# Three batches of attention as one list of steps, and one quad's row sums moved from TensorE to VectorE

## The chip, the cores and the metric

The kernel runs on one core of a Trainium2 chip. The metric is device microseconds from launch to end; the profile gives the time from the first to the last instruction of one execution, called the span.

## The reference

Cosine attention over 8 batches, 12 heads, 448 positions and 64 features, and behind it a two-layer feed-forward block with an exact GELU on the 3584 x 768 result:

```python
q_n = q / (np.linalg.norm(q, axis=-1, keepdims=True) + 1e-06)
k_n = k / (np.linalg.norm(k, axis=-1, keepdims=True) + 1e-06)
scores = np.matmul(q_n, k_n.transpose(0, 1, 3, 2)) / tau
attn = np.exp(scores - scores.max(-1, keepdims=True))
attn = attn / (attn.sum(-1, keepdims=True) + 1e-09)
x = np.matmul(attn, v).transpose(0, 2, 1, 3).reshape(B * S, H * D)
h = x @ w_in                                  # 768 -> 2048
out = (0.5 * h * (1.0 + erf(h / sqrt(2)))) @ w_out    # 2048 -> 768
```

The kernel leaves the subtraction of the maximum out: scores of unit vectors divided by 0.1 stay small enough. Inputs and output are float32; the matrix products run in bfloat16 and add up in float32.

## The kernel before

Four heads are a *quad*: three quads a batch, 24 in all, numbered g. Heads lie in pairs on the 128 partitions, and the 448 positions are seven chunks c of 64. A *unit* is what is normalised at once: units 0 and 1 are the halves of quad 0, and unit u from 2 on is quad u - 1. `load_qk(g)` loads a quad's q and k, so unit 5 belongs to `load_qk(4)`.

For each unit: `square` (ScalarE or GpSimd), `reduce` to sums of squares (VectorE), `logs` and `roots` (ScalarE, a square root as exponential of half a logarithm), `inverses` (VectorE), `scale` (GpSimd, gives bfloat16), `transposes` (TensorE with `copies` by VectorE for units 0 to 4, a DMA transpose on SP's queue for the others). Units share their logs and roots in groups; from group 5 on a group is not a unit.

For each quad and chunk: `scores` (four 64x64 matmuls side by side in the array, tile `st`), `exps` (ScalarE, 896 columns, line 252), the sums over rows, and `values` (four matmuls a chunk, tile `o`). `visit(p)` is one chunk's scores and exponentials in bank pair p. The sums come in three ways: `sums`, matmuls against ones into tile `sm`, followed by `turned` and `inverted`; `folded`, additions by GpSimd into SBUF; and `gathered`, additions by VectorE into a bank pair; the last two are followed by `turned_all` and `inverted_all`. `spread` and `normalise` (VectorE) then give x, bfloat16.

For each batch: `first(b)` projects x with `w_in` (96 matmuls of 448 columns, tile `hp`) and applies `gelu` on ScalarE from each bank. The second product (tile `op`, 16 matmuls of 384 columns for each half row block) is cut into single matmuls, *pieces*, which the next batch's attention takes in between its own work; the 16th copies the bank out, and a finished block is stored from SP's queue.

A program order is written out by hand (`manual_schedule`): each engine and each queue runs its instructions in the order in which the code issues them. Buffers are reused in that order too: q and k have four, v two, PSUM two single banks (`mm`, taken in turn for `tp`, `sm`, `op` and some `hp`), two pairs `st0`, `st1`, and two more single banks that become a third pair after batch 0.

Batch 0's attention is a list (`attention_first`); those of batches 1 and 2 are branches in `attention(b, fill)`, with a list `parts` of how many pieces go into each place; the rest is one pattern. `late_copy`, before the change two plain lines, is a copy of one column of quad 0's last load by GpSimd, ahead of its first other work. `spin` matmuls are padding: TensorE computes something that nothing reads.

Of the kernel before, what the change touches and what calls it, by code (L numbers as in the profile page):

```python
# [9 lines left out]
F32 = mybir.dt.float32  # L10
# [6 lines left out]
def kernel(  # L17
# [108 lines left out]
    def load_qk(g):  # L126
        b, n = divmod(g, NQ)
        t = qkp.tile([128, 2, 2, C, D], F32, tag="qk", name=f"qk{g}")
        qk_t[g] = t
        for s0, s1 in ((0, 1), (1, 2)) if g == 0 else ((0, 2),):  # L130
            for i, src in enumerate((q, k)):
                eng = nc.scalar if g == 0 and s0 == 0 and i == 1 else nc.sync
                eng.dma_start(
                    out=t[:, i, s0:s1].rearrange("p s c d -> p s (c d)"),
                    in_=src[b, 4 * n + 2 * s0:4 * n + 2 * s1].rearrange(
                        "(s h) (p c) d -> (h p) s (c d)", h=2, c=C))
# [127 lines left out]

    def gathered(g, p):
# [58 lines left out]
    def values(g, chunks=range(C), p=None):  # L324
        for c in chunks:
            if c == 0 and g < NQ:
# [70 lines left out]
    def second_pieces(sb, t, ni):  # L397
        state = {}

        def mm(kf):  # L400
# [8 lines left out]
            if kf == KF - 1:  # L409
                nc.vector.tensor_copy(ot[:, ni * NH:(ni + 1) * NH], ps[:, :NH])  # L410
# [7 lines left out]
        return [lambda kf=kf: mm(kf) for kf in range(KF)]  # L418
# [46 lines left out]
    early = {}  # L465

# [5 lines left out]
    def attention_first():  # L472
        x_t[0] = xp.tile([128, KD, S], BF16, tag="x", name="x0")
        DV, AC, GP = nc.vector, nc.scalar, nc.gpsimd
        Q, K = 0, 1
        square(0, ((AC, Q),))
        square(0, ((AC, K),))
        reduce(0, Q)
        reduce(0, K)
        square(1, ((AC, Q),))  # L480
        upto(load_v, 1)
        logs(0)
        reduce(1, Q)
        roots(0)
        upto(load_wi, 1)
        square(1, ((AC, K),))
        inverses(0)
        square(2, ((AC, Q),))
        reduce(1, K)
        scale(0, ((GP, 1),))  # L490
        logs(1)
        reduce(2, Q)
        roots(1)
        scale(0, ((GP, 0),))
        spin(2)
        transposes(0, 1)
        square(2, ((AC, K),))
        inverses(1)
        spin(1)
        transposes(0, 0)  # L500
        square(3, ((AC, Q),))
        copies(0, 1)
        scale(1, ((GP, 0),))
        copies(0, 0)
        square(3, ((AC, K),))
        scale(1, ((GP, 1),))
        upto(load_qk, 5)
        spin(1)
        transposes(1, 0)
        reduce(2, K)  # L510
        scores(0, ((0, 0), (0, 1)))
        upto(load_v, 2)
        transposes(1, 1)
        copies(1, 0)
        logs(2)
        scores(0, ((0, 2), (0, 3)))
        roots(2)
        upto(load_wi, 2)
        exps(0, ((0, 0), (0, 1)))
        inverses(2)  # L520
        copies(1, 1)
        exps(0, ((0, 2), (0, 3)))
        spin(2)
        scores(0, ((0, 4), (0, 5)))
        scale(2, ((GP, 0),))
        reduce(3, Q)
        exps(0, ((0, 4), (0, 5)))
        spin(1)
        scores(0, ((1, 0), (1, 1)))
        reduce(3, K)  # L530
        exps(0, ((1, 0), (1, 1)))
        spin(1)
        scores(0, ((1, 2), (1, 3)))
        scale(2, ((GP, 1),))
        upto(load_qk, 6)
        transposes(2, 0)
        exps(0, ((1, 2), (1, 3)))
        sums(0, (0,))
        copies(2, 0)
        scores(0, ((1, 4), (1, 5)))  # L540
        logs(3)
        scores(0, ((0, 6), (1, 6)))
        roots(3)
        transposes(2, 1)
        exps(0, ((1, 4), (1, 5)))
        inverses(3)
        sums(0, (1,))
        scale(3, ((GP, 0),))
        copies(2, 1)
        sums(0, (2,))  # L550
        exps(0, ((0, 6), (1, 6)))
        sums(0, range(3, 5))
        scores(1, ((0, 0), (1, 0)))
        scores(1, ((0, 1), (1, 1)))
        sums(0, (5,))
        exps(1, ((0, 0), (1, 0)))
        sums(0, (6,))
        upto(load_wi, 3)
        transposes(3, 0)
        turned(0)  # L560
        exps(1, ((0, 1), (1, 1)))
        scores(1, ((0, 2), (1, 2)))
        values(0, (0,))
        scale(3, ((GP, 1),))
        upto(load_wi, 4)
        copies(3, 0)
        values(0, (1,))
        exps(1, ((0, 2), (1, 2)))
        values(0, (2,))
        scores(1, ((0, 3), (1, 3)))  # L570
        inverted(0)
        values(0, range(3, 5))
        spread(0, 1)
        values(0, (5,))
        exps(1, ((0, 3), (1, 3)))
        scores(1, ((0, 4), (1, 4)))
        values(0, (6,))
        spread(0, 0)
        sums(1, (0,))
        square(4, ((GP, K),))  # L580
        exps(1, ((0, 4), (1, 4)))
        sums(1, (1,))
        scores(1, ((0, 5), (1, 5)))
        normalise(0, 0)
        transposes(3, 1)
        exps(1, ((0, 5), (1, 5)))
        scores(1, ((0, 6), (1, 6)))
        copies(3, 1)
        sums(1, (2,))
        square(4, ((GP, Q),))  # L590
        square(5)
        upto(load_wo, 2)
        exps(1, ((0, 6), (1, 6)))
        sums(1, range(3, 5))
        normalise(0, 1)
        scores(2, ((0, 0), (1, 0)))
        sums(1, (5,))
        exps(2, ((0, 0), (1, 0)))
        sums(1, (6,))
        scores(2, ((0, 1), (1, 1)))  # L600
        turned(1)
        values(1, range(2))
        exps(2, ((0, 1), (1, 1)))
        values(1, (2,))
        scores(2, ((0, 2), (1, 2)))
        inverted(1)
        values(1, range(3, 5))
        spread(1, 0)
        values(1, (5,))
        exps(2, ((0, 2), (1, 2)))  # L610
        values(1, (6,))
        scores(2, ((0, 3), (1, 3)))
        sums(2, (0,))
        reduce(4, K)
        normalise(1, 0)
        exps(2, ((0, 3), (1, 3)))
        sums(2, (1,))
        scores(2, ((0, 4), (1, 4)))
        spread(1, 1)
        values(2, (0,))  # L620
        sums(2, (2,))
        exps(2, ((0, 4), (1, 4)))
        scores(2, ((0, 5), (1, 5)))
        normalise(1, 1)
        values(2, range(1, 3))
        exps(2, ((0, 5), (1, 5)))
        values(2, (3,))
        scores(2, ((0, 6), (1, 6)))
        exps(2, ((0, 6), (1, 6)))
        reduce(4, Q)  # L630
        spin(1)
        early[4] = mm_tile("hp0_4")[:, :S]
        w_in(0, early[4], 4, range(2))
        sums(2, range(3, 7))
        values(2, (4,))
        logs(4)
        turned(2)
        values(2, (5,))
        roots(4)
        values(2, (6,))  # L640
        inverted(2)
        inverses(4)
        scale(4)
        spread(2, 1)
        spread(2, 0)
        normalise(2, 1)
        normalise(2, 0)
        done.update({square: 6, reduce: 5, root: 5, scale: 5, transposes: 5})

# [49 lines left out]

    def attention(b, fill):
        fill = list(fill)
        if b == 1:
            parts = iter((20, 13, 14, 17, 16, 16))
        elif b == 2:
            parts = iter((22, 12, 12, 13, 11, 13, 11, 11, 11, 6, 6))
        elif len(fill) == 128:
            parts = iter((14, 22, 22, 26, 28, 16))
        else:  # L710
            parts = iter((14, 17, 13, 18, 18, 16))
# [28 lines left out]
        if b == 1:  # L740
            upto(scale, u + 3)
            upto(load_v, b + 2)
            upto(transposes, u + 3)
            upto(load_qk, g0 + NQ + 2)
            upto(square, u + 4)
            visit(0, 1, 2)
            run()
            visit(0, 1, 2)
            run()
            upto(load_qk, g0 + NQ + 3)  # L750
            visit(0, 1)
            upto(square, u + 5)
            run()
            visit(0, 1, 2)
            both(g0, 0)
            upto(load_v, b + 3)
            upto(load_qk, g0 + NQ + 4)
            visit(1, 2)
            upto(reduce, u + 4)
            run()  # L760
            visit(1, 2, 0)
            both(g0 + 1, 1)
            visit(2, 0)
            logs(6)
            roots(6)
            run()
            both(g0 + 2, 2)
            inverses(6)
            done[root] = 7
        elif b == 2:  # L770
            upto(scale, u + 3)
            upto(load_qk, g0 + 6)
            upto(transposes, u + 3)
            upto(scale, u + 4)
            upto(load_qk, g0 + 7)
            upto(transposes, u + 4)
            visit(0, 1, 2)
            run()
            visit(0, 1, 2)
            norms(9)  # L780
# [230 lines left out]
```

## Time and profile before

| | |
|---|---|
| times of three runs | 402.37, 400.3, 406.49 us (median 402.37) |
| span of the profiled execution | 398.6 us |
| its own time | not among the three; the lowest run is 1.7 us above its span |
| TensorE, VectorE, ScalarE, GpSimd busy | 98, 66, 67, 63% |
| granted TensorE clock | 0.999 |

A row of the costliest groups reads: line, engine, operation, written tile <- read tiles, shapes, count | busy us, mean ns of one | idle us of that engine just before them, and what ended most of that. Rows of the chain are start, length, what. In a timeline the bracket at a row's end says how long the engine was idle before it, and for what.

### The profile page before, as it was taken

What the parts mean: (1) busy time and instruction counts of PE and PEld (TensorE: products, weight loads), DVE (VectorE), ACT (ScalarE), POOL (GpSimd) and SP (SyncE); (2) the same over time, 40 slices, a digit from 0 to 9 for tenths busy, and PEclk for the clock granted to TensorE, in tenths of its full rate; (3) what the DMA queues carried; (4) which work ended last, traced back from release to release, by engine and by line L of the source; (5) the groups of instructions that cost most, each with busy time, mean ns of one, the idle gap of its engine ahead of it and who ended that gap; (6) DMA issues with size and microseconds to landing.
All of it is one profiled execution on the core that took longest, in us unless ns stands there. A gap on an engine that the chain in (4) does not pass through costs nothing.

```text
span 398.6 us, 8027 instructions
## 1 busy us (share of the span) xinstructions
PE 392.0 (98%) x3245; PEld 207.8 (52%) x3245; DVE 264.0 (66%) x530; ACT 267.8 (67%) x399; POOL 250.6 (63%) x162
## 2 busy tenths in 40 slices
PE   7999999999999999999999999999999999999996
PEld 3444555555545555555555555555555555555564
DVE  5787214955487999589963999769973797461021
ACT  6995787557988877888665977889656756504300
POOL 5898814269699694959587394969768391920000
PEclk9999999999999999999999999999999999999999
DMA  8999999747296890678145591566024720130033
GB/s 290 261 258 217 205 233 308 154 106 226 50 254 234 158 230 2 178 150 207 70 105 138 126 240 38 162 113 147 2 27 101 148 46 2 41 77 3 1 80 80
DMA packets 66485, 54.52 MB, mean 137 GB/s; under 512 B 38672, under 2 KB 62352, under 8 KB 66448
## 3 DMA queue, kind: packets, MB, share of 16 engines
q1 hardware_dynamic: 54464, 41.79, 39.0%
q0 software_dynamic: 11600, 11.80, 18.8%
q8 instruction: 25, 0.41, 0.4%
q10 hardware_dynamic: 384, 0.43, 0.3%
q14 instruction: 12, 0.10, 0.1%
HBM read 45.61 MB, written 11.01 MB: 142 GB/s over the span
## 4 chain that ended last, share of the span: by engine, by line
PE 95%; issue 1%; DVE 1%; POOL 1%; ACT 0%; POOLq 0%
PE hp L469 37%; PE op L406 36%; PE st L242 9%; PE o L320 4%; PE o L335 4%; PE op L425 1%; PE sm L305 1%; PE sh L667 1%; PE tp L221 1%; PE sm L314 1%; PE spin L463 0%; POOL wi L441 0%; DVE nq L168 0%; POOL qkb L204 0%; POOL v L145 0%
## 5 line engine op out<-in xcount | busy, mean ns | idle before, releaser
L252 ACT ACTIVATE pt<-st 128x896 bf16<-128x896 f32 x155 | 132.5, 916 | 29.0 <-PE st L242 28.4
L406 PE MATMUL op<-wo,g 128*128 128x384 bf16 x864 | 148.1, 326 | 0.0
L469 PE MATMUL hp<-x,wi 128*128 128x448 bf16 x768 | 147.0, 353 | 0.1
L204 POOL TENSOR_TENSOR qkb<-qk,rn 128x896 bf16<-128x896 f32 (+1 forms) x50 | 80.2, 1628 | 66.3 <-DVE rn L188 64.9
L406 PEld LDWEIGHTS <-g 128*128 128x128 bf16 x864 | 81.4, 98 | 62.6 <-issue 11.2
L469 PEld LDWEIGHTS <-wi 128*128 128x128 bf16 x768 | 74.4, 98 | 71.1 <-issue 2.8
L263 POOL TENSOR_TENSOR acc<-acc,pt 128x896 f32<-128x896 f32 x55 | 103.8, 1887 | 4.3
L929 ACT ACTIVATE g<-hp 128x448 bf16<-128x448 f32 x128 | 63.6, 552 | 63.6 <-PE hp L469 63.5
L410 DVE COPY ot<-op 128x384 f32<-128x384 f32 x54 | 29.9, 555 | 83.1 <-PE op L406 80.8
L168 DVE TENSOR_REDUCE nq<-sq 128x14 f32<-128x896 f32 (+1 forms) x50 | 50.6, 1038 | 10.2 <-POOL sq L160 6.7
L242 PE MATMUL st<-qkT 64*64 64x448 bf16 x620 | 46.0, 356 | 0.2 <-ACT pt L252 0.2
L160 POOL TENSOR_TENSOR sq<-qk 128x896 f32<-128x896 f32 x18 | 29.9, 1683 | 16.3 <-DMA qk<-in_q_dram 10.9
L369 DVE TENSOR_TENSOR x<-o,rs 128x448 bf16<-128x448 f32 x48 | 28.0, 609 | 9.9 <-PE sh L667 6.4
L270 DVE TENSOR_TENSOR acc<-acc,pt 128x896 f32<-128x896 f32 x30 | 33.0, 1099 | 1.0
L158 ACT ACTIVATE sq<-qk 128x896 f32<-128x896 f32 (+1 forms) x32 | 27.8, 902 | 2.2 <-DMA qk<-in_q_dram 1.8
L364 DVE STREAM_TRANSPOSE rs<-rc 128x448 f32<-128x448 f32 x48 | 28.7, 626 | 0.6
L242 PEld LDWEIGHTS <-qkT 64*64 64x64 bf16 x620 | 17.9, 105 | 20.5 <-issue 12.7
L263 POOL TENSOR_TENSOR acc<-pt 128x896 f32<-128x896 bf16 x11 | 20.7, 1879 | 8.9 <-DVE x L369 8.9
L320 PE MATMUL o<-pt,v 64*64 64x448 bf16 x364 | 24.2, 351 | 0.0
L673 ACT ACTIVATE pt<-sh 128x448 bf16<-128x448 f32 x26 | 14.1, 544 | 9.2 <-PE sh L667 8.5
L276 DVE STREAM_TRANSPOSE ta<-acc 128x448 f32<-128x448 f32 x32 | 18.5, 617 | 0.2
L335 PE MATMUL o<-pt,v 64*64 64x448 bf16 x308 | 17.5, 351 | 0.5 <-DVE x L369 0.5
(54 smaller groups left out, 212.4 us busy)
## 6 DMA issues: line engine op xcount, KB each, us to landing
qk<-in_q_dram SPq DMA_DIRECT2D x23, 448.0 KB, 4.6
qk<-in_k_dram SPq DMA_DIRECT2D x23, 448.0 KB, 5.4
out_dram<-ot SPq DMA_DIRECT2D x48, 192.0 KB, 3.2
v<-in_v_dram POOLq DMA_DIRECT2D x7, 672.0 KB, 7.7
wo<-in_moe_w_out_dram POOLq DMA_DIRECT2D x4, 768.0 KB, 11.6
wi<-in_moe_w_in_dram POOLq DMA_DIRECT2D x4, 512.0 KB, 14.4
out_dram<-ot SPq DMA_DIRECT2D x12, 96.0 KB, 2.1
wi<-in_moe_w_in_dram POOLq DMA_DIRECT2D x4, 256.0 KB, 14.6
```

The source lines that it names most:

```text
L160: eng.tensor_tensor(sq, t, t, ALU.mult)
L168: nc.vector.tensor_reduce(nq_t[n][:, j, i], sq_t[g, i][:, s0:s1], mybir.AxisListType.X, ALU.add)
L204: eng.tensor_tensor(qkb[:, i, :, s0:s1].rearrange("p c s d -> p s c d"), t[:, i, s0:s1], rn[:, i].to_broadcast([128, s1 - s0, C, D]), ALU. ...
L242: nc.tensor.matmul(st[cols, n, :S], lhsT=qkT[rows, 1, c, cols], rhs=qkT[rows, 0, :, cols], start=True, stop=True, tile_position=(64 * s, 6 ...
L252: nc.scalar.activation(pt, st[:, :, :S], AF.Exp, scale=inv_tau)
L263: nc.gpsimd.tensor_tensor(acc_t[g], all_t[g][:, 0] if c == 1 else acc_t[g], all_t[g][:, c], ALU.add)
L270: nc.vector.tensor_tensor(acc_t[g], acc_t[g], all_t[g][:, c], ALU.add)
L320: nc.tensor.matmul(bank_t[g, h][64 * s:64 * (s + 1), :S], lhsT=v_t[g][rows, s, c, :], rhs=pt_t[g, s, c][rows], start=(c == 0), stop=(c == ...
L335: nc.tensor.matmul(bank_t[g, h][cols, :S], lhsT=v_t[g][rows, s, c, :], rhs=pt_t[g, s, c][rows], start=(c == 0), stop=(c == C - 1), tile_po ...
L406: nc.tensor.matmul(ps[:, :NH], lhsT=g_t[sb][:, kf, t * 128:(t + 1) * 128], rhs=wo[:, kf, ni * NH:(ni + 1) * NH], start=(kf == 0), stop=(kf ...
L469: nc.tensor.matmul(t, lhsT=wi[:, kd, m * 128:(m + 1) * 128], rhs=x_t[b][:, kd, :], start=(kd == 0), stop=(kd == KD - 1))
L929: nc.scalar.activation(g_t[sb][:, m, hf * S:(hf + 1) * S], hps.pop(m), AF.Gelu)
```

## The change

Batches 0, 1 and 2 up to `first(2)` become one list, `opening()`; `first(0)`, `first(1)` and the branches for batches 1 and 2 go, and the remaining code loses what only they used. What the list changes for the engines:

- `sums(3)`, the row sums of quad 3 by TensorE, becomes `gather(3, c)`, six VectorE additions into an SBUF tile, with `turned_all` and `inverted_all`.
- 8 of 14 copies of `op` banks in batches 1 and 2 go from VectorE to ScalarE (`run(1, AC)`).
- Squares: unit 1 from ScalarE to GpSimd; unit 5, one half each of units 6, 7, 9 and 10 from GpSimd to ScalarE; one half of unit 13 the other way.
- GpSimd's queue: the parts of `w_in`, issued before the scaling of quads 0, 1 and 2, go behind it; `late_copy` goes from the front to behind `load_wi(2)`; `load_v(4)` comes ahead of `load_v(3)`.
- SP's queue: `load_qk(10)` before 9 and 8, and stores in other places.
- The chunks of quads 0 to 2 come in another order, single matmul groups of batches 1 and 2 in other places; the 29 `spin` matmuls are placed one by one but for one run of 20; the two matmuls `early` are no longer taken ahead.

```diff
+    def gather(g, c):
+        if c == 1:
+            acc_t[g] = sqp.tile([128, 2, S], F32, tag="sq", name=f"acd{g}")
+        nc.vector.tensor_tensor(acc_t[g], all_t[g][:, 0] if c == 1 else acc_t[g], all_t[g][:, c], ALU.add)
...
-        def mm(kf):
+        def mm(kf, eng):
...
-                nc.vector.tensor_copy(ot[:, ni * NH:(ni + 1) * NH], ps[:, :NH])
+                (nc.scalar.copy if eng is nc.scalar else nc.vector.tensor_copy)(ot[:, ni * NH:(ni + 1) * NH], ps[:, :NH])
...
+    def run(n, eng=nc.vector):
+        for _ in range(n):
+            todo_t.pop(0)(eng)
...
+        square(1, ((GP, Q),))
...
+        scale(3, ((GP, Q),))
+        turned(0)
...
+        load_wi(2)
+        load_qk(4)
+        sums(1, (1,))
+        late_copy()
...
+        values(2, (3,))
+        values(2, (4,))
+        exps(2, ((0, 5), (1, 5)))
+        sums(2, (2,))
+        sums(2, (3,))
+        sums(2, (4,))
+        sums(2, (5,))
+        sums(2, (6,))
+        load_wi(3)
+        values(2, (5,))
+        values(2, (6,))
...
+        mm(0, 3, 0, 4)
...
+        table(GELU_SET)
+        bank(0, 5)
+        square(5, ((AC, K),))
+        mm(0, 4, 4, 6)
+        gelu(0, 4)
...
+        gather(3, 2)
+        run(1)
+        gather(3, 3)
+        gather(3, 4)
+        reduce(7, K)
+        gather(3, 5)
+        run(2)
+        gather(3, 6)
+        run(1)
+        run(1, AC)
...
+        sums(4)
+        turned(4)
...
+        load_v(4)
+        run(2)
+        table(GELU_SET)
+        inverted(5)
+        spread(5, 0)
+        load_v(3)
...
+        gelu(1, 13)
+        inverses(7)
+        bank(1, 11)
+        square(9, ((AC, Q),))
+        gelu(1, 12)
...
+    opening()
+    assert not todo_t, len(todo_t)
+    first(2)
+    for b in range(3, B):
+        attention(b, output_pieces(b - 1))
+        first(b)
```

## The prediction

> **What bounds the kernel now.** I read the page first: span, busy shares, the chain that ended last, the costliest groups.
>
> ```profile
> span 398.6 us, 8027 instructions
> PE 392.0 (98%) x3245; PEld 207.8 (52%) x3245; DVE 264.0 (66%) x530; ACT 267.8 (67%) x399; POOL 250.6 (63%) x162
> ...
> PE 95%; issue 1%; DVE 1%; POOL 1%; ACT 0%; POOLq 0%
> ...
> L252 ACT ACTIVATE pt<-st 128x896 bf16<-128x896 f32 x155 | 132.5, 916 | 29.0 <-PE st L242 28.4
> ...
> L929 ACT ACTIVATE g<-hp 128x448 bf16<-128x448 f32 x128 | 63.6, 552 | 63.6 <-PE hp L469 63.5
> L410 DVE COPY ot<-op 128x384 f32<-128x384 f32 x54 | 29.9, 555 | 83.1 <-PE op L406 80.8
> ```
>
> TensorE is 95% of the chain, and the other engines wait for it, not it for them. A busy TensorE need not be a fast one, so next the chain in order of time (start, length, what).
>
> ```profile
> 31.09 0.88 PE sm L305 x8
> 31.96 0.69 PE o L335 x12
> 32.65 8.81 PE hp L469 x46
> 41.46 0.78 PE tp L221 x14
> ...
> 51.33 0.69 PE st L242 x12
> ...
> 76.93 0.78 PE sm L314 x16
> 77.70 1.45 PE o L335 x28
> 79.15 18.29 PE hp L469 x96
> 97.44 0.69 PE st L242 x12
> 98.13 3.68 PE op L406 x22
> ...
> 102.50 2.06 PE op L406 x12
> ...
> 151.71 2.28 PE op L406 x14
> ```
>
> 18.29 us / 96 is 0.190 us for a matmul of 448 columns; 22 against 12 `op` matmuls is (3.68 - 2.06)/10 = 0.162 us for one of 384 columns and 0.12 us for starting the group. 448/384 times 0.162 is 0.189, so both stream at one rate, and from 32.65 us on the pieces follow each other with next to nothing between. There only TensorE work that goes away, or a new stall, can move the end. Before 32.65 us it is otherwise; the windows (width, then busy us of PE, PEld, DVE, ACT, POOL) and ScalarE's timeline show it:
>
> ```profile
> 12.30:32.65 20.35, 19.61 (x242) 8.58 (x239) 15.38 (x27) 19.48 (x27) 18.44 (x16) 1.00 1.09 255
> 51.30:66.00 14.70, 14.70 (x137) 7.49 (x136) 2.23 (x4) 11.93 (x14) 4.38 (x3) 1.00 1.18 283
> 97.40:133.45 36.05, 36.05 (x386) 18.56 (x386) 24.20 (x53) 33.23 (x44) 27.91 (x18) 1.00 0.71 180
> ```
>
> ```profile
> 12.29 4.13 ACT L252 ACTIVATE pt<-st 128x896 bf16<-128x896 f32 x5
> ...
> 18.66 10.29 ACT L252 ACTIVATE pt<-st 128x896 bf16<-128x896 f32 x12 [0.16 <-PE st L242]
> 29.49 1.73 ACT L252 ACTIVATE pt<-st 128x896 bf16<-128x896 f32 x2 [0.55 <-PE st L242]
> 31.10 0.32 ACT L175 ACTIVATE lq<-nq,tiny 128x28 f32<-128x28 f32 x1
> ```
>
> From 12.29 to 31.1 us ScalarE runs the first batch's 21 exponentials, 10.29/12 = 0.857 us each, almost without a break: it bounds the opening.
>
> **The change, part by part.** From the third batch's projection (`first(2)`) on, both kernels run the same steps from the same state: 77 score tiles are done by then in both, and the same loads, squares and scales. So the 246.9 us after 151.71 us stand as they are, and I sum what happens before.
>
> *Sums of quad 3.* `sums(3)` goes: 16 matmuls, 0.78 us on TensorE (the row at 76.93 us), from a stretch that TensorE bounds: **-0.78**. VectorE takes six additions `gather(3, c)` and the long form of the inversion instead. No row has an addition with both inputs in SBUF; nearest are the six of `gathered`, whose running sum lies in PSUM, and GpSimd's additions with the same two operands:
>
> ```profile
> L263 POOL TENSOR_TENSOR acc<-acc,pt 128x896 f32<-128x896 f32 x55 | 103.8, 1887 | 4.3
> ...
> L168 DVE TENSOR_REDUCE nq<-sq 128x14 f32<-128x896 f32 (+1 forms) x50 | 50.6, 1038 | 10.2 <-POOL sq L160 6.7
> ...
> L270 DVE TENSOR_TENSOR acc<-acc,pt 128x896 f32<-128x896 f32 x30 | 33.0, 1099 | 1.0
> ```
>
> I take 1.10, same engine and shape; 1.89 is the upper end, 1.04, VectorE's reduction of as many elements, the lower. The rest, transposes to reciprocal, ran from 146.72 to 150.96 us in `first(2)`; the second row gives the exponentials of quad 3:
>
> ```profile
> 146.72 1.18 DVE L276 STREAM_TRANSPOSE ta<-acc 128x448 f32<-128x448 f32 x2
> ...
> 150.63 0.33 DVE L294 RECIPROCAL rc<-su 128x28 f32<-128x28 f32 x1
> ```
>
> ```profile
> 53.22 5.05 ACT L252 ACTIVATE pt<-st 128x896 bf16<-128x896 f32 x6
> ```
>
> In the new order VectorE does, in one piece, six additions, a `reduce` and these 4.24 us: 6 x 1.10 + 1.04 + 4.24 = 11.9, then the copy of an `op` bank (0.56). It can begin when the second exponential of quad 3 is done, two of 0.84 after 53.22, less 0.2 because batch 0's projection now ends at 51.1 instead of 51.33 (below): 54.7. So that copy is done at 67.1. Who waits: `sums(4)` takes its bank. TensorE is there after 72 `op` (11.7 us), 17 score tiles at 0.69/3 (3.9), one `values` (1.45) and six starts (0.7): 51.1 + 17.8 = 68.9. **Slack 1.8 us, cost 0**; at 1.89 us an addition the copy is at 71.8 and costs 2.9.
>
> The Trainium skill, "SBUF — State Buffer", "Who interferes with whom", speaks against this part: a VectorE instruction with two SBUF inputs and a GpSimd instruction that reads SBUF shut each other out for a whole instruction. No row here shows it, as no VectorE operation of this kernel has two such inputs. GpSimd is busy 4.38 of 14.70 us there (window 51.30:66.00), so by the rule each of the six additions would meet an instruction of 1.7 us with a chance of 0.3 and wait half of it: 1.5 us, within the slack on average and beyond it where they meet badly.
>
> *The opening.* ScalarE gives the two squares of unit 1 to an idle GpSimd, but its first exponential also waits for VectorE's reductions of quad 1, which stand in the same order; I leave 12.29 and the 21 exponentials. Behind the last one stood 8 sums and 12 values (0.88 + 0.69 = 1.57 us, the rows at 31.09 and 31.96); now two chunks' sums (4 matmuls, 0.44) and two of values (8, 0.46): **-0.66**. Bounds: another -0.55 if the wait at 29.49 us goes too, 0 if an exponential comes that much later. Two `hp` matmuls that ran in that hole return to the stream: 2 x 0.190 = **+0.38**. The padding `spin` matmuls are 29 as before and stand in holes: 0.
>
> *Loads.* GpSimd now issues each part of `w_in` behind the scaling that used to follow it, and `load_qk(4)` waits for `late_copy`, since that reads the buffer it fills and stands on GpSimd behind `load_wi(2)`. In the old trace that place is 23.5 us, and the load went out at 11.29:
>
> ```profile
> 20.58 1.72 POOL L204 TENSOR_TENSOR qkb<-qk,rn 128x896 bf16<-128x896 f32 x1
> 22.22 1.26 POOL L441 DMA_DIRECT2D wi<-in_moe_w_in_dram  x2
> ```
>
> ```profile
> L133 SPq DMA_DIRECT2D qk<-in_k_dram x1: 471/471/471, 11.7 to 11.7; - x1
> ...
> DMA to landing us min/median/max: 10.5/11.5/12.5
> ```
>
> ```profile
> L133 SPq DMA_DIRECT2D qk<-in_k_dram x1: 471/471/471, 17.0 to 17.0; - x1
> ...
> DMA to landing us min/median/max: 12.5/14.8/17.0
> ```
>
> ```profile
> L133 SPq DMA_DIRECT2D qk<-in_k_dram x1: 491/491/491, 88.3 to 88.3; - x1
> ...
> DMA to landing us min/median/max: 3.8/4.1/4.4
> ```
>
> `k` of load 4, issued at 24.0, lands between 28.4 (4.4, free queues) and 41.0 (17.0). ScalarE's `square(5, K)` needs it and stands ahead of the first `gelu`. TensorE asks for that gelu's bank after 30 `hp` matmuls and 7 transposes, 32.0 + 30 x 0.190 + 0.4 = 38.1; less a gelu (0.55), a square (0.90) and a handover (0.2), the load must have landed by 36.4, 12.4 us after its issue. The load of 17.0 us stood behind the one that landed at 11.7 + 12.5 = 24.2 and took 9.8 us from there. Nothing is ahead of load 4 now, so I take 10 us, 34.0: **cost 0**, upper bound 4.6. Loads 5 and 6 stand behind it on SP; their squares come 5 to 10 us later. The parts of `w_in`, 3 to 5 us later than before, have their first users from 32.0 on, the last at about 39: the same cover, the same bound.
>
> ```profile
> 86.10 1.50 SPq L216 DMA_TRANSPOSE qkT<-qkb  x1
> ```
>
> A second wait of this kind: `load_v(3)` now comes behind `load_v(4)` and waits on GpSimd for `values(5)`, and `load_qk(9)` on SP waits behind a store of about the same time. `values(5)` ends at 68.9 + `sums` 0.8 + four score tiles 0.9 + 11 `op` 1.9 + two `values` 2.9 = 75.4. Behind stand `square(10, K)` and `scale(7, Q)` (1.7 each, as the row at 20.58), the DMA transpose (1.5), `load_qk(8)` (4.4) and ScalarE's `square(9, Q)`, ahead of `gelu(1, 12)`: with 6 us for load 9, 75.4 + 6 + 3.4 + 1.5 + 4.4 = 90.7. TensorE asks for that gelu's bank after 0.8 + 13 `op` 2.1 + 78 `hp` 14.8 + starts 0.5, at 93.6, so the load must be there by 93.6 - 0.55 - 0.90 - 0.2 = 91.9: cost 0, and 2.8 if load 9 takes 10 us.
>
> *TensorE's groups.* `op` and score matmuls change places 19 times instead of 18 up to `first(2)`, and unit 4's transposes are two groups: 2 x 0.12 = **+0.23**, from the start of a group above. The Trainium skill, "TensorEngine Tiling (Array Packing)", "Key Properties", says that a change of tiling mode drains the array; the 0.12 us agrees with a drain of that size, and by the rule the same two changes count.
>
> *ScalarE in batches 1 and 2.* It takes 8 of the 14 `op` copies. No row has that copy; by elements it is 384/448 of a gelu's 0.552 = 0.47, at most a whole one. In 51.30:66.00 it has 2.77 us free for three. In 97.40:133.45, the tightest, 36.05 - 33.23 = 2.82 us are free; five copies less one square given to GpSimd are 5 x 0.47 - 0.90 = 1.45. Score tiles wait for a bank that an exponential frees, so part of it reaches TensorE: between 0 and 1.45, and half, **+0.7**, as half the free time goes. The squares that ScalarE takes in the two projections lie in its waits for `hp` (63.5 us in all).
>
> *The sum:* -0.78 - 0.66 + 0.38 + 0.23 + 0.70 = **-0.13 us** on a span of 398.6, to 398.5. The profiled execution's own time is not among the three shown; their median, 402.37, is 3.8 us above its span and their lowest, 400.3, 1.7. I put the change on the median: **402.2 us**.
>
> **The rivals.**
> *Faster by 1.4 us (401.0):* -0.78 - 0.66 - 0.55 + 0.38 + 0.23, the opening in full and no loss on ScalarE. For it: ScalarE's copies may fall into its waits for `st` (28.4 us in the page). Against it: nothing else is left to win, as TensorE streams.
> *Slower by late transfers, the other side:* `k` of load 4, with `square(5, K)` ahead of the first gelu. It decides from a landing at 36.4 us and costs what is beyond, up to 4.6: 402.2 + 4.6 = 406.8. For it: 17.0 us is a row of this queue. Against it: that row includes waiting for an earlier load.
> *Slower by VectorE:* the `op` copy late at `sums(4)`, from additions of 1.4 us on (1.10 + 1.8/6). At 1.89 us it costs 2.9. If the three GpSimd instructions beside them (`scale(6, K)` and the squares of unit 8, 1.7 us each) hold VectorE up once each, 5.1 - 1.8 = 3.3: 405.5. For it: no row has such an addition. Against it: GpSimd is idle most of that stretch. The rule of the Trainium skill quoted above would make the second price.
> *The change does not act:* the sums of quad 3 stay off TensorE in any case, but if ScalarE eats all of its 1.45 and the opening gives 0, the sum is -0.78 + 0.38 + 0.23 + 1.45 = +1.3: 403.6. This is in the forecast's own range.
>
> **How the numbers follow.** Forecast 0.55, faster rival 0.13, late transfers 0.17, VectorE 0.15. The range: low 398.5, the faster rival less the 2.1 us that the lowest run lies below the median, rounded down; high 409, late transfers with some 2 us of the runs' scatter on top. 2% is 8 us, about what a measurement of this kernel can tell from no change. Faster by that has no source (the whole hole before 32.65 us is not 8 us, as ScalarE fills it): 0.02. Slower by it needs both slow rivals in full (4.6 + 3.3 = 7.9) and more: 0.07. The rest, 0.91, is within 2%.
>
> **What would show it.** The first long run of `hp` begins near 32.0 us; `hp` of batch 1 ends near 97; no `sm` rows between 76 and 79 us more than two quads' in batch 1. L270's counterpart in `gather` shows 1.1 us. Wrong if TensorE's busy time falls clearly below the span between 32 and 152 us: a wait of `hp` for a gelu near 38 us (late transfers), of `sm` for an `ot` copy near 69 us (VectorE), or of `st` for `pt` between 100 and 133 us beyond 1.45 us (ScalarE).

## The result, and the profile after

The changed kernel takes 403.27 us (median of 17 runs, 400.63 to 406.33), the kernel before 400.79 beside it: a ratio of **1.0055, 95% interval 1.0031 to 1.008**. It is a little slower: 2.5 us by the medians, where my sum said 0.13 us less. The time lies in my range; the change is clear of the noise and goes the other way. The profiled execution has a span of 401.4 us against 398.6; its own time is 403.13.

First the page of the changed kernel: span, busy times, the chain by engine, and the groups of `hp` matmuls and score tiles.

```profile
span 401.4 us, 8020 instructions
PE 392.5 (98%) x3229; PEld 207.7 (52%) x3229; DVE 268.7 (67%) x533; ACT 273.1 (68%) x410; POOL 244.0 (61%) x159
...
PE 87%; DVE 3%; DMA 3%; ACT 3%; issue 1%; SPq 1%; POOL 0%; DVEq 0%; ACTq 0%; POOLq 0%
...
L472 PE MATMUL hp<-x,wi 128*128 128x448 bf16 x768 | 147.9, 353 | 1.7 <-ACT g L501 1.7
...
L242 PE MATMUL st<-qkT 64*64 64x448 bf16 x620 | 46.5, 357 | 1.4 <-ACT ot L415 0.9
```

TensorE is still 98% busy, but the chain no longer runs through it alone: DMA, ScalarE and VectorE hold 9% of it, and two idle stretches of 1.7 and 0.9 us stand in rows that had 0.2 us at most before. The chain in order of time shows where:

```profile
1.94 0.55 PE spin L468
2.53 0.55 PE spin L468
...
3.71 5.96 PE spin L468 x20
9.71 0.55 PE tp L221 x7
...
32.57 3.89 PE hp L472 x20
...
67.39 0.41 DVE ot L415
...
76.53 8.47 DMA qk<-in_k_dram
...
86.78 1.69 POOL qkb L204
88.49 1.50 SPq L216
90.03 4.04 DMA qk<-in_q_dram
94.15 0.95 ACT sq L158
95.10 0.44 ACT g L501
95.58 1.29 PE hp L472 x6
...
99.31 0.69 PE st L242 x12
...
136.29 18.16 PE hp L472 x96
```

The last rows answer to 97.44 and 133.45 us of the kernel before. From `first(2)` on, the two run alike.

| stretch, by the chains | before | after | difference |
|---|---|---|---|
| start to the first long run of `hp` | 32.65 | 32.57 | -0.08 |
| to batch 2's first score tile | 64.79 | 66.74 | +1.95 |
| to `first(2)` | 36.01 | 36.98 | +0.97 |

So the opening gives nothing of its 0.66 us, batches 0 and 1 lose instead of gaining, and batch 2 loses 1. In the second stretch stands a wait of `hp` for a gelu, in the third one of score tiles, and there the matmuls and their weight loads name different causes (waits of PE, and of PEld, TensorE's weight loads: us in total, times, longest):

```profile
PE hp L472 <- ACT g L501: 1.7, 1, 1.7
PE st L242 <- ACT ot L415: 0.9, 1, 0.9
...
PEld L242 <- DMA qkT<-qkb: 1.3, 1, 1.3
```

### The profile page after: what moved, and what is told of

Read it like the earlier page. It is cut to its first block, busy times and chain, and to the rows that moved or that the text cites. A ratio compares the mean times of both kernels' runs of the same rounds, so it can differ in the third digit from the quotient of the medians.

```text
span 401.4 us, 8020 instructions
## 1 busy us (share of the span) xinstructions
PE 392.5 (98%) x3229; PEld 207.7 (52%) x3229; DVE 268.7 (67%) x533; ACT 273.1 (68%) x410; POOL 244.0 (61%) x159
## 4 chain that ended last, share of the span: by engine, by line
PE 87%; DVE 3%; DMA 3%; ACT 3%; issue 1%; SPq 1%; POOL 0%; DVEq 0%; ACTq 0%; POOLq 0%
PE hp L472 33%; PE op L411 32%; PE st L242 8%; PE o L325 4%; PE o L340 3%; PE spin L468 2%; DMA qk<-in_k_dram 2%; ACT pt L252 2%; DVE acd L268 1%; PE op L430 1%; PE sm L310 1%; PE tp L221 1%; PE sh L518 1%; DMA qk<-in_q_dram 1%; ACT sq L158 0%
## 5 line engine op out<-in xcount | busy, mean ns | idle before, releaser
L415 DVE COPY ot<-op 128x384 f32<-128x384 f32 x46 | 25.5, 554 | 65.0 <-PE op L411 62.7
L160 POOL TENSOR_TENSOR sq<-qk 128x896 f32<-128x896 f32 (+1 forms) x15 | 23.6, 1581 | 32.7 <-DMA qk<-in_q_dram 17.5
L158 ACT ACTIVATE sq<-qk 128x896 f32<-128x896 f32 (+1 forms) x35 | 31.7, 930 | 7.5 <-DMA qk<-in_q_dram 5.6
L325 PE MATMUL o<-pt,v 64*64 64x448 bf16 x364 | 24.2, 351 | 0.0
```

Of the source, the lines that this page charges most:

```text
L158: eng.activation(sq, t, AF.Square)
L325: nc.tensor.matmul(bank_t[g, h][64 * s:64 * (s + 1), :S], lhsT=v_t[g][rows, s, c, :], rhs=pt_t[g, s, c][rows], start=(c == 0), stop=(c == ...
```

## The experiments

My theory after this: three things went wrong beside the sums, and independently. Single padding matmuls lengthen the block at the start; load 9 (`load_qk(9)`) takes 8.5 us, and a square on ScalarE that waits for the load behind it holds up the gelus; in batch 2 a DMA transpose comes late. The rival for the last is ScalarE, with its copies of `op` banks. Unless another kernel is named, each edit is made to the changed kernel, and no edit changes what is computed.

### The padding at the start (e1, e12)

```diff
-        spin(1)
         x_t[0] = xp.tile([128, KD, S], BF16, tag="x", name="x0")
...
-        spin(1)
-        spin(1)
         square(1, ((GP, K),))
         reduce(0, Q)
-        spin(20)
+        spin(22)
```

> The changed kernel with the first 23 padding matmuls as one group of 22, as before the change, instead of three single ones and a group of 20. Theory (each single one pays for its own bank and wait, 0.59 us, and the group then ends after the first scaling): the group ends near 8.3 us, the first transposes come near 8.65 instead of 9.71, the first exponential near 12.3 instead of 13.33, the long run of hp near 31.5 instead of 32.5, the span is 1.0 us shorter than the changed kernel's 401.4. Rival (the first exponential waits for VectorE's reduction of unit 2 in any case, or the sums behind the last exponential set the end of the opening): the transposes come earlier, but the hp run begins within 0.3 us of 32.5 and the span stays within 0.4 us of 401.4.

Median 402.2 us, ratio to before 1.0031 (1.002 to 1.0042); span 398.9. TensorE in e1's timeline:

```profile
1.95 5.88 PE L468 MATMUL spin<-g,ident 128*128 128x448 bf16 x22 [1.95 <-DVE root L92]
8.51 0.58 PE L221 MATMUL tp<-ident,qkb 128*64 128x128 bf16 x7 [0.68 <-POOL qkb L204]
...
31.76 3.96 PE L472 MATMUL hp<-x,wi 128*128 128x448 bf16 x20
...
119.62 0.76 PE L242 MATMUL st<-qkT 64*64 64x448 bf16 x12 [0.97 <-DMA qkT<-qkb]
```

The transposes come at 8.51, and `hp` 0.74 us earlier than in the changed kernel (31.76 against 32.50 in the same view). The span is 2.5 us shorter, not 1.0, because the wait for the gelu is missing too: `k` of load 9 landed 5.4 us after its issue here, not 8.5. That transfer differs from execution to execution, so one profile can't price the padding. With the other two waits mended in both (below), e12 keeps the three single matmuls:

> The three edits without the one on the padding: the three single padding matmuls are kept. Theory: the opening is 0.75 us longer, nothing behind it changes, since the waits for transfers are gone: span 0.7 to 0.8 us above the kernel with the three edits. Rival (the earlier arrival is taken up by a wait further on): within 0.2 us of it.

The median is 400.80 against 400.12 without them (e10, beside it on one chip): +0.68, as expected. But e12's profiled execution, its fastest run, has a span of 398.1, with `hp` from 31.40 on as without them. The padding alone in windows (width, busy us and matmuls begun or running), first of the changed kernel, then of e12:

```profile
5.20:6.70 1.50, 1.50 (x6) 1.00 1.05 363
6.70:8.20 1.50, 1.50 (x7) 1.00 1.05 388
```

```profile
5.20:6.70 1.50, 1.50 (x9) 1.00 1.02 366
6.70:8.20 1.50, 1.50 (x10) 1.00 1.05 398
```

In the first microseconds a matmul takes twice its time, 0.37 instead of 0.19 us from start to start (the clock column, 1.00 here, does not show it), and when that ends differs between executions of the same opening: near 7.8 us in the changed kernel's, 5.3 in e12's. What the single matmuls cost (0.59 us apart instead of 0.37, so 3 x 0.22 = 0.66) is hidden when the rate doubles early and shows when it doubles late: the first transposes come at 8.50 us in e12, at 9.71 in the changed kernel, and in no profile here before 8.50, as they wait for GpSimd's first scaling (e1's row). Where the rate doubles at about the same time, 6.4 us in e8 (below) without the three and 6.5 in e9 with them, they come at 8.51 and 9.05.

### The late load in batch 1 (e2, e9, e5)

```diff
-        square(10, ((GP, K),))
...
         scale(7, ((GP, Q),))
+        square(10, ((GP, K),))
```

> The changed kernel with scale(7, Q) and its DMA transpose ahead of square(10, K) on GpSimd. Theory (GpSimd stands 8 us behind load 9, and with it the scaling that frees the buffer of load 8, so that square(9, Q) on ScalarE and with it the gelu behind it come 1.7 us late): scaling near 77, load 8 issued near 81 instead of 90.0, no wait of hp for a gelu at 95.6, span 401.4 - 1.7 = 399.7. Rival (load 8 lands no earlier because it now shares the queues with load 9 and two loads of v, or another wait takes its place): load 8 lands after 92 all the same, and the span falls by less than 0.8.

Median 403.38, ratio 1.0077 (1.0057 to 1.0097), span 403.1: no gain on the changed kernel, and the theory's number missed. SP's and TensorE's rows, and TensorE's clock in windows (the last three numbers are clock, DMA share, GB/s):

```profile
79.10 7.12 SPq L216 DMA_TRANSPOSE qkT<-qkb  x1
86.26 0.58 SPq L133 DMA_DIRECT2D qk<-in_q_dram  x1
```

```profile
95.69 5.19 PE L472 MATMUL hp<-x,wi 128*128 128x448 bf16 x18 [2.25 <-ACT g L501]
```

```profile
95.60:97.00 1.40, 1.31 (x4) 0.55 (x4) 1.40 (x2) 1.40 (x5) 1.40 (x1) 0.50 1.06 393
97.00:98.40 1.40, 1.40 (x5) 0.59 (x4) 1.31 (x2) 0.65 (x2) 0.18 (x1) 0.50 1.03 326
```

The transpose was issued at 79.10 instead of 88.49, and then held SP for 7.12 us, with load 9 under way; load 8 got out at 86.26, and its q landed near 94. This is the rival's outcome. And in this execution the stall of 2.25 us cost more than itself: behind it the granted clock is 0.50, and 18 `hp` matmuls take 5.19 us, where they take 3.73 after the changed kernel's stall of 1.68. The other three runs of e2 have a mean clock of 0.999 or 1.0, so the median does not hold this cost.

The other way is to give load 9 the transfer engines alone:

```diff
-        load_v(4)
...
-        load_v(3)
...
         scale(8, ((GP, Q),))
+        load_v(4)
+        load_v(3)
```

> The changed kernel with load_v(4) and load_v(3) on GpSimd behind scale(8, Q) instead of ahead of square(10, K). Theory (load 9 takes 8.5 us because it shares the transfer engines with two loads of v, 672 KB each, that GpSimd issues at the same time; the load at 88 us of the kernel before, alone, took 4.4): k of load 9 lands within 5 us of its issue, the square behind it begins near 81 instead of 85, load 8 lands near 90, no wait of hp for a gelu at 94, span 401.4 - 1.7 = 399.7. Rival (it is slow behind the four stores on its own queue): it lands 8 us after its issue as before, the stall stays, span 401.4.

`k` of load 9 landed after 5.3 us, and the gelus did not wait. But beside the loads of v as they were it took 5.4 to 8.9 in twelve profiled executions, so one landing of 5.3 fits the theory and does not settle it. What speaks for it: in the two shortest, 5.4 (e1) and 6.0 (e10), load 9 was issued 0.33 us or more ahead of the first load of v; in the other ten, 7.5 to 8.9, by 0.24 at most, or behind it. The loads of v now meet load 11 and unit 8's DMA transpose, which took 15.0 us, and score tiles waited for it:

```profile
L216 SPq DMA_TRANSPOSE qkT<-qkb x1: 7183/7183/7183, 94.2 to 94.2; - x1
...
DMA to landing us min/median/max: 15.0/15.0/15.0
```

```profile
109.18 0.96 PE L242 MATMUL st<-qkT 64*64 64x448 bf16 x8 [5.26 <-DMA qkT<-qkb]
```

Median 406.16, ratio 1.013 (1.011 to 1.015). The wait and a spell at half clock behind it (last section) are both in this (mean clock 0.992 to 0.996 in all four runs). What helped was to leave the transfers alone and move what waits for them:

```diff
-        square(9, ((AC, Q),))
         gelu(1, 12)
...
         gelu(1, 14)
+        square(9, ((AC, Q),))
```

> The changed kernel with ScalarE's square(9, Q), which waits for load 8, behind the last gelu of batch 1's projection instead of ahead of gelu(1, 12). Loads, scalings and transposes stay where they are. Theory (that square is the only thing through which the late loads reach TensorE in batch 1): no wait of hp for a gelu near 94 us, batch 1's hp ends 1.7 us earlier, span 401.4 - 1.7 = 399.7 and less scatter between executions. Rival (the late load only moves the wait: unit 9's reduce, logs, scaling and DMA transpose come later by the same time, and score tiles of batch 2 wait for them): the stall at 94 goes, a new one of 1 to 2 us comes between 115 and 125, span at 401 or above.

```profile
81.65 15.30 PE L472 MATMUL hp<-x,wi 128*128 128x448 bf16 x80
...
120.46 0.76 PE L242 MATMUL st<-qkT 64*64 64x448 bf16 x12 [0.90 <-ACT ot L415]
```

80 `hp` matmuls in one piece, no stall; median 401.71, ratio 1.0012 (0.9984 to 1.004), span 399.8 as the theory had it. The wait at 120 is the one that was at 122.

### The stall in batch 2 (e3, e6, e4)

```diff
-        square(12, ((GP, Q),))
...
         scale(10, ((GP, K),))
         transposes(10)
+        square(12, ((GP, Q),))
```

> The changed kernel with square(12, Q) behind scale(10, K) and the DMA transpose of unit 10 on GpSimd instead of ahead of it. Theory (the 0.9 us in which score tiles stand still at 122 us end with the landing of that DMA transpose): it is issued near 112.8 instead of 114.5, lands 1.5 us earlier, the stall at 122 goes, span 401.4 - 0.9 = 400.5. Rival (the stall ends with ScalarE's copy of an op bank, behind a square that ScalarE got too): the transpose lands earlier, the stall stays at 0.8 to 0.9 us, span 401.4.

Span 401.9, median 403.46 (1.0032 to 1.0175 of before), and the stall grew to 1.70 us. Neither theory had that. Unit 10's DMA transpose went out 1.9 us earlier and landed later; its own issue in the changed kernel, in e3 and in e6 (below):

```profile
L216 SPq DMA_TRANSPOSE qkT<-qkb x1: 2953/2953/2953, 114.5 to 114.5; - x1
DMA to landing us min/median/max: 7.5/7.5/7.5
```

```profile
L216 SPq DMA_TRANSPOSE qkT<-qkb x1: 5610/5610/5610, 112.6 to 112.6; - x1
DMA to landing us min/median/max: 9.9/9.9/9.9
```

```profile
L216 SPq DMA_TRANSPOSE qkT<-qkb x1: 1501/1501/1501, 113.9 to 113.9; - x1
DMA to landing us min/median/max: 3.5/3.5/3.5
```

In e3, as in the changed kernel, `load_qk(13)` stands straight ahead of it on SP; `scale(10, K)` frees the buffer that this load waits for, so both went out 1.9 us earlier together. In e6 the load stands behind it:

```diff
-        load_qk(13)
...
         transposes(11)
+        load_qk(13)
```

> The changed kernel with load_qk(13) behind the DMA transposes of units 10 and 11 on SP instead of ahead of them. Theory (a DMA transpose that is issued with a load under way on the same queue takes 7 to 8 us for two instead of 1.5 to 2.6 each, so that unit 10's lands after TensorE has come to its first score tile): the transpose is issued near 113.5, lands before 119, the stall of 0.9 us at 122 goes, span 401.4 - 0.9 = 400.5. Rival ScalarE (the stall ends with its copy of an op bank): the stall stays, span 401.4.

Landing after 3.5 us instead of 7.5, and no wait of score tiles above 0.2 us. Batch 2 goes from 99.63 to 135.54 us in e6's timeline, 35.91, against 36.01 before the change, with all of ScalarE's copies in place. The median is 401.47 (0.9951 to 1.0025); the gelu still waits 1.46 in its profile.

The rival, ScalarE's copies, was tried directly (three of the five `run(1, AC)` of batch 2 become `run(1)`):

> The changed kernel with three of batch 2's five op copies on ScalarE, the one ahead of the stall at 122 us among them, back on VectorE. Theory late transpose: the copy at 121.5 is done elsewhere, and the score tiles still start near 122.0, span 401.4 (to 401.2). Rival ScalarE: the stall of 0.9 us at 122 us goes, span 400.5; if the copies cost 0.7 in all, as I had it for five, three give 0.4 back.

```profile
PE st L242 <- DVE x L374: 3.5, 3, 3.1
PE op L411 <- DVE tr L348: 2.2, 1, 2.2
```

```profile
120.07 0.56 DVE ot L415
...
121.62 0.57 DVE tr L348
```

Median 409.89, ratio 1.0225 (1.02 to 1.025), and neither theory had that. The second fence is from the chain: VectorE, which takes its work in order, stands idle for 5.6 us before the copy at 120.07, until TensorE has filled the bank, and a reduction and the transposes of the row sums stand behind the copy. TensorE waits for these transposes, and later for `normalise`. So e4 shows that the copies cost more on VectorE in these places; that ScalarE's copies are not what TensorE waits for at 122 us, e6 shows.

### The three mended together (e7, e10, e8, e11)

e1's, e5's and e6's edits in one kernel:

> The three edits together: first padding as one group of 22, square(9, Q) behind the last gelu, load_qk(13) behind the DMA transposes of units 10 and 11. Theory: the three stalls are all that the list lost, and what it won (16 sums matmuls, 0.78 us) shows: span 401.4 - 0.75 - 1.7 - 0.9 = 398.0, median near 399.9, 0.2% below the kernel before, executions within 1 us. Rival (other waits come forward once these are gone, as TensorE arrives earlier): span 399 or above, not faster than the kernel before.

Median **399.95 us, ratio 0.9967 (0.9943 to 0.9991)**. The same kernel again, for its profile:

> The kernel with the three edits once more, for its profile beside the kernel before on one chip, and against the two variants that run with it: span 398.0 to 398.8, first long run of hp near 31.4, batch 1's hp to 96.5, first(2) near 132.6, that is 0.6 us below the kernel before at each of the three places or more.

Median 400.12, ratio 0.9983 (0.9973 to 0.9992), runs from 399.81 to 400.75. By both measurements this kernel is 0.2 to 0.3% faster than the kernel before, a small gain, and clear of the noise. TensorE in its timeline:

```profile
31.35 3.96 PE L472 MATMUL hp<-x,wi 128*128 128x448 bf16 x20
...
96.08 0.76 PE L242 MATMUL st<-qkT 64*64 64x448 bf16 x12
...
100.29 0.75 PE L242 MATMUL st<-qkT 64*64 64x448 bf16 x8
101.47 0.38 PE L242 MATMUL st<-qkT 64*64 64x448 bf16 x4 [0.43 <-ACT pt L252]
...
132.83 7.35 PE L472 MATMUL hp<-x,wi 128*128 128x448 bf16 x38
```

Against the same places of the kernel before (32.59, 97.37 and 133.38 us in its timeline) the opening gains 1.24 us, the stretch from there to batch 2 only 0.05, and batch 2 loses 0.74: a gain of 0.55 in all. The opening carries it; what leaving out `sums(3)` saves goes to the two `hp` matmuls that the stream got back, to group starts and to a wait of 0.22 us for VectorE. Batch 2 loses its time at 100 to 104 us, 0.8 us of waiting score tiles, since the moved square stands ahead of their exponentials: that is what its place costs. e11 puts the square behind three of these exponentials:

> The three edits, but square(9, Q) behind the first three exponentials of batch 2 instead of ahead of them. In the kernel with the three edits score tiles wait 0.43 us near 102 for an exponential that stands behind this square. Theory: that wait goes and nothing takes its place, as ScalarE then has the time of 20 op pieces: 0.4 us below the kernel with the three edits, span 397.6. Rival: unit 9's logs and scaling come 2.5 us later, and its DMA transpose then arrives late: 0.5 us or more above.

Slower, as on the rival's side, but by another way: 405.35, ratio 1.0128 (1.0092 to 1.0165). VectorE's reduction of that square stands ahead of the copy of an `op` bank, and TensorE waits for the copy:

```profile
105.28 0.32 PE L411 MATMUL op<-wo,g 128*128 128x384 bf16 x1 [2.09 <-DVE ot L415]
```

At last the gain itself, with quad 3's sums back on TensorE in the mended kernel:

```diff
-        gather(3, 1)
...
-        turned_all(3)
+        sums(3)
+        turned(3)
...
-        inverted_all(3)
+        inverted(3)
```

> The kernel with the three edits, and quad 3's row sums on TensorE again (sums, turned, inverted, in the place of the VectorE additions). Theory: 16 matmuls more for TensorE, 0.78 us plus 0.1 for one more group, all on its path: span 0.9 us above the kernel with the three edits. Rival (the additions cost VectorE, and TensorE behind it, as much as the matmuls): spans within 0.3 us of each other.

Median 401.63 against e7's 399.95, run beside it: +1.7. In its profile `sums(3)` waits 1.06 us for a bank that ScalarE's copy frees, so the place that I gave it is not a good one. 1.7 less 1.06 leaves 0.6: the 0.78 of the matmuls, less a wait of 0.22 us for VectorE (near 69.5 in e10) that e8 has not. So the additions win in this kernel, and cost 0.2 us of what they save.

## Why the prediction was wrong

Three steps failed, each in its own stretch: the padding of the opening and the second late load, both put at 0, and the DMA transpose of batch 2, which has no term.

**Sums of quad 3: right.** The additions took 1.09 us each (1.10), the `op` copy was done at 67.80 (67.1), `sums(4)` came at 69.12 (68.9). So the slack was 1.3 us, not 1.8, and the cost 0. The five additions to the running sum:

```profile
L268 DVE TENSOR_TENSOR acd<-acd,pt 128x896 f32<-128x896 f32 x5 | 5.5, 1090 | 0.4
```

Whether the Trainium skill's rule of "SBUF — State Buffer", "Who interferes with whom", would have made them longer no run here shows: GpSimd was idle from 53.7 to 66.3 us in the changed kernel, and during the additions of every other profile too.

**Opening: wrong at "29 as before and stand in holes: 0".** I counted the padding matmuls and not how they are issued. The first exponential, which I left at 12.29 us, came at 13.33 in the changed kernel, behind padding that ended at 9.7. In e10, without the three single ones, the first `hp` comes 1.24 us earlier than before the change, my -0.66 with the further -0.55 that I gave as its bound. In the changed kernel they and a late doubling of TensorE's rate took all of it; how late it is, is luck, and no term of mine had it.

**Load 4: cost 0 as forecast, but by luck, as two errors cancelled.** In the list `load_qk(4)` stands ahead of `late_copy`, not behind it as I had read. It went out at 17.73 us, as GpSimd's scaling of quad 1 ended, not at 24.0; the load that went out just behind `late_copy`, at 24.42, is load 6. `k` of load 4 took 14.5 us, not 10, and landed at 32.6, before 36.4.

**The second wait: the chain was right, its size wrong.** `load_qk(9)`, `square(10, K)`, `scale(7, Q)`, the DMA transpose, `load_qk(8)`, `square(9, Q)`, gelu: all in the chain, with load 9 issued at 75.9 (75.4). But I set the load at 6 us, "cost 0, and 2.8 if load 9 takes 10", and then put no rival on it. Its `k` took 8.47, and the wait was 1.68; with 8.47 in place of 6 the same chain gives 93.2 - 91.9 = 1.3. Why the load is so slow stays open: e9 and the order of issue speak for the loads of v beside it.

**TensorE's groups: half of the +0.23 was not there.** From the first `hp` to the end of batch 0's projection the chains have 19.06 us against 18.68: the 0.38 of two `hp` matmuls, and nothing for a second group of transposes. Their rows and those of `hp` are both 128*128, so no change of tiling stands between them.

**ScalarE in batch 2: wrong, +0.70 where e6 shows -0.10 for the batch.** My total for batch 2 looked right by accident: its loss of 0.97 was the DMA transpose behind `load_qk(13)`, an issue that had changed places on SP and that I had not followed.

**Rivals.** "Late transfers" had the mechanism, but at load 4 instead of loads 9 and 13. The forecast's sum had none of the three losses: each stood at 0 in it, or not at all.

## What to carry to other kernels

When a program order changes, list for each queue which transfer now stands ahead of which, and price a load by the slowest row of a shared queue where others are issued beside it; a wait whose slack is near 1 us deserves a rival of its own. If transfers are late, first move the instruction that waits for them, for moving transfers moved the collision (e2 and e3 gained nothing, e9 lost). One profile of a kernel that races its loads is one draw: look at medians and at which waits differ between executions.

## What the runs showed of the hardware

**A DMA transpose behind a load was slow in these runs.** Unit 10's landed 3.5 us after its issue without a load straight ahead of it on SP (e6), 7.5 and 9.9 with one (the changed kernel, e3), and held SP for 2.95 and 5.61 us instead of 1.50; unit 8's, with a load straight ahead and two loads of v under way, took 15.0 (e9).

**Behind a stall of some 2 us TensorE's clock can halve.** After 2.25 us (e2) and 5.26 us (e9) the granted clock is 0.50 for some 3.4 us, which costs up to 1.7. After 2.20 in e4 it stays at 1.00, and after 1.79 in e3 too (the last number but two is the clock):

```profile
95.30:97.00 1.70, 1.68 (x9) 0.79 (x9) 1.64 (x2) 1.70 (x5) 1.11 (x1) 1.00 1.05 354
```

The place of the stall counts. By the traces' record of the granted clock, the spells begin at 95.60 us (e2), 108.87 (e9), 108.29 (e11) and 127.35 (e4, behind a wait of 3.08), and these are 26, 30, 30 and 35 times 3.413 us after the rate first doubled (6.85, 6.47, 5.89, 7.88). Of the 3.41 us ahead of a spell TensorE was idle for 1.92 (e11) to 3.41 (e9). The 1.79 us of e3 lie in one such stretch, and e4's 2.20 are cut in two, 1.71 at most in one. So the length of a stall alone does not decide; which share of a stretch must be idle stays open.

Four of the 17 runs of the changed kernel, 404.55 to 406.33 us, have a mean clock of 0.995 to 0.996: one such spell in 400 us would give 1 - 1.7/400 = 0.996. They have no profile, so this is an inference.

The Trainium skill, "TensorE: Matmul & The Clock Gate", "Part 1: The HAM clock gate (the "warmup" mystery)", tells of a free-running window of 3413 ns after which the rate doubles or halves, and warns of idle gaps above some 3.4 us. The traces agree on the half rate at the start, its end at another time in each execution, and spells of that length, a whole number of them behind the first doubling; on the gap the measurement decides: 2.25 us was enough in e2.
